# Attention, GLU and SoLU layers on one core: small tiles in a pool of their own, and the next block's q turned earlier from other slots

## The chip, the cores and the metric

The kernel runs on one core of a Trainium2 chip. The metric is the device time of one execution in microseconds (us); before the change the median of three runs is 1464.21 us (1464.13 to 1465.03). A core has TensorE (PE, matrix products; PEld is its loading of the stationary operand), VectorE (DVE), ScalarE (ACT), GpSimd (POOL), and SyncE (SP), whose queue issues nearly all DMA transfers here. A matrix product has a stationary operand ("weights", 128 columns) and a moving operand (up to 512 columns).

## What is computed

Three layers one behind the other, in float32 with float64 weights for the last two:

```python
q_s = exp(q - max(q, axis=-1));  q_s /= sum(q_s, axis=-1) + 1e-9      # q, k, v: 8 x 8 x 576 x 64
k_s = exp(k - max(k, axis=2));   k_s /= sum(k_s, axis=2) + 1e-9
kv  = einsum('bhsd,bhse->bhde', k_s, v)
x   = einsum('bhsd,bhde->bhse', q_s, kv)     # put together as 4608 tokens x 512
g   = x @ w_gate;  y = (g * sigmoid(g) * (x @ w_val)) @ w_out         # 512 -> 1536 -> 512
h   = y @ w_in;    s = h * softmax(h)                                 # 512 -> 1024
out = ((s - mean(s)) / sqrt(var(s) + 1e-6) * g_ln) @ w_out2           # 1024 -> 512
```

Each large product is made of three matrix products: an operand is split into a high and a low part (names ending in h and l), and high·high, high·low and low·high are summed.

## The kernel before

**Stages.** The 4608 tokens are ten blocks (`BLOCKS`): blocks 0 and 1 of 288 tokens run in a start-up stage that a clock of due times orders (until about 190 us), blocks 2 to 8 of 512 tokens and block 9 of 448 run in a hand-written order (`block`, 190 to 1050 us), and the last layer runs over 36 tiles of 128 tokens (`rest`, `emit_h`, `emit_out`, from about 1053 us).

**A block.** It has 36 gaps, three for each of the 12 columns i of w_gate and w_val. In gap 3i stands `emit_g` (12 products `wg`, then Silu on ACT), in gap 3i+1 the output product of the column before (`next_o`, 12 products `y`), in gap 3i+2 `emit_v` (12 products `wv`, then `v_rest`: multiply on DVE, L851; high part on ACT, L855; low part on DVE, L857). The engines work their instructions off in program order. `tasks_of(j)` puts further tasks into the gaps, behind the block's own work of that gap: k and v of the same block j (`kv_load`, `v_load`, `kv_max_rows`, `kv_max_all`, `kv_exp`, `kv_mm`, in two halves of four heads, the second half 12 gaps behind the first), and q of the next block (`q_max` 8, `q_exp` 12, `q_norm` 20, `q_turn` 24, `q_split` 27 to 30, `x_mm` 29 to 32). `x_mm` makes the next block's x in four parts, each of which starts with three or six products `px` (six where the block's tokens lie in two of the eight batches).

**Turning q.** `q_turn` (L647) copies the low and high halves of q's words into the tile `qw` (DVE L652, ACT L653), and a transposing DMA (L655) writes `qwT`, from which `q_split` (L659) puts together z (DVE and ACT, L664) and its parts qh (ACT L669) and ql (DVE L670). `qw` lies in the slot of k (`kt`), `qwT` in that of v (`vt`); both have one buffer, so `q_turn` stands behind the second half's `kv_mm` in gap 23. k, v and q for the next block are loaded together in gap 32 (`load_next`, L765), q by one transfer for each head and batch (16 where a block lies in two batches).

**Weights.** Columns 0 to 4 and 9 to 11 are loaded again for every block by `stream_next` in gap 3f+2, and in gap 25 for column 11 (three slots in turn: a0, a3, a4); each load waits until the products that used its slot are through, and is used nine gaps later. Columns 5 to 8 (`wgv5` to `wgv8`) and all of w_out stay; `wgv4` to `wgv8`, `wo2` and `wo3` were first loaded into tiles b0 to b6 of the pool `wb`, and `wo5` took b0 from `wgv4`. One `wo` tile serves two columns. So of the 432 products of 512 columns in a block, those with weights in `wb` are 4 × 24 for `wgv5` to `wgv8` and 6 × 12 for `wo2`, `wo3` and `wo5`: 168.

**Where the tiles lie.** Pools follow each other in each partition's bytes: const, w, x, a, tmp, att, and behind att first att0, later wb, later late2. Nearly all tiles are multiples of 512 bytes. Behind const's small tiles everything starts at byte 224 modulo 512: all tiles of w, x, a, tmp and those of k, v and q. In att the tiles qm, qs and rs (640 bytes) put qh and ql at 352 modulo 512, and m, r, r2 and r3 (1184 bytes) put z, and all of wb, at 0. In late2 (last layer), nm, se, ss, nmu, sv and rstd put zh and zl at 64. wb starts at byte 170496 of the partition; all tiles at 224 end below 158432.

**y_fix** (L776, blocks 3 to 6) adds two halves of y of the start-up blocks in a tile `fix` in the slot `yt`, which the end of a block's output (`emit_o`, gap 4 of the next block) uses too.

Of the kernel before, what the change touches and what calls it, by code (L numbers as in the profile page):

```python
# [9 lines left out]
F32 = mybir.dt.float32  # L10
# [9 lines left out]
P = 128  # L20
# [97 lines left out]
def attention_glu_solu_kernel(  # L118
# [23 lines left out]
    nc = tc.nc  # L142
# [28 lines left out]

    const = ctx.enter_context(tc.tile_pool(name="const", bufs=1))
    dram = ctx.enter_context(tc.tile_pool(name="dram", bufs=1, space=DRAM))
    wpool = ctx.enter_context(tc.tile_pool(name="w", bufs=1))

    ident = const.tile([P, P], F32, name="ident")
# [246 lines left out]

    def kv_max_rows(pool, b, h0):
        raw = kt_t[b, h0][0]
        km_t[b, h0] = m = pool.tile([SP, HG, D], F32, tag="m", bufs=1, name="m")
        nc.vector.tensor_reduce(
            out=m, in_=raw.rearrange("p c h d -> p h d c"), axis=AX.X, op=ALU.max
        )

    def kv_max_all(pool, b, h0, split=0):

        raw, kt = kt_t[b, h0]
        m = km_t.pop((b, h0))
        kt_sub.add((b, h0))
        N = HG * D
        NQ = SP // 32
        r = pool.tile([SP, N // 32], F32, tag="r", bufs=1, name="r")
        nc.vector.tensor_reduce(
            out=r, in_=m.rearrange("p h (e j) -> p (h e) j", j=32), axis=AX.X, op=ALU.max,  # L440
            apply_transpose=True,
        )
        r2 = pool.tile([32, N // 32, NQ], F32, tag="r2", bufs=1, name="r2")
        for a in range(NQ):
            nc.vector.tensor_copy(out=r2[:, :, a], in_=r[32 * a:32 * (a + 1), :])
        r3 = pool.tile([32, N // 32], F32, tag="r3", bufs=1, name="r3")
        nc.vector.tensor_reduce(out=r3, in_=r2, axis=AX.X, op=ALU.max)
        mb = tmp.tile([SP, N // 32, 32], F32, tag="st", bufs=3, name="mb")
        for a in range(NQ):
            nc.vector.tensor_copy(  # L450
                out=mb[32 * a:32 * (a + 1)],
                in_=r3.rearrange("p (n o) -> p n o", o=1).to_broadcast([32, N // 32, 32]),
            )
        mt = pool.tile([SP, 1, HG, D], F32, tag="m", bufs=1, name="mt")
# [68 lines left out]
    def kv_mm(ps, pool, b, h0, u):  # L523
        kt, vt = kt_t[b, h0][1], vt_t[b, h0]
        pr = h0 // 2 + u
        need(pr in k_done if b == 0 else (b, h0) in kt_exp)
        pk = ps.tile([P, D + 1], F32, tag="gv", name="pk")
        for c in range(KC):
            for a in range(2):
                nc.tensor.matmul(  # L530
                    out=pk[a * D:(a + 1) * D, :],
                    lhsT=kt[:, c, 2 * u + a, :],
                    rhs=vt[:, 2 * u + a, c, 0:D + 1],
                    start=(c == 0),
                    stop=(c == KC - 1),
                )
        yield d["rs"]
        hi, lo = kv_parts[b % 2, pr]
        rs = pool.tile([P, 1], F32, tag="rs", bufs=4, name="rs")
        nc.vector.tensor_scalar_add(out=rs, in0=pk[:, D:D + 1], scalar1=1e-9)  # L540
        nc.vector.reciprocal(out=rs, in_=rs)
        yield d["kvh"]
        diag = [slice(a * D, (a + 1) * D) for a in range(2)]
        for s in diag:
            nc.scalar.activation(out=hi[s, s], in_=pk[s, 0:D], func=AF.Copy, scale=rs[s])
        yield d["kvl"]
        for s in diag:
            nc.vector.scalar_tensor_tensor(
                out=lo[s, s], in0=pk[s, 0:D], scalar=rs[s], in1=f32(hi[s, s]),
                op0=ALU.mult, op1=ALU.subtract,  # L550
            )
        kv_done.add((b, pr))
# [13 lines left out]
    def q_load(pool, j, raw_pool=None, tag="qt"):  # L566
        b, half = divmod(j, 2)
        if j >= 2:
            x = pool.tile([BLOCKS[j][1] // 4, 4, H, D], F32, tag=tag, bufs=1, name=tag)
            for b, s, ps in segments(j):  # L570
                for h in range(H):
                    nc.sync.dma_start(
                        out=x[ps, :, h, :],
                        in_=q[b, h, s:s + 4 * (ps.stop - ps.start), :]
                        .rearrange("(p c) d -> p c d", c=4),
                    )
            qt_t[j] = x, x
            return
        qt_t[j] = heads_load(
# [10 lines left out]
    def q_max(pool, j, hs):  # L590
# [2 lines left out]
        placed(qt_t, j)  # L593
        raw, qt = (t[:, :, hs, :] for t in qt_t[j])
        n, nc_, nh = qt.shape[:3]
        qm = pool.tile([n, nc_, nh, 1], F32, tag="qm", bufs=2, name="qm")
# [10 lines left out]
    def q_norm(pool, j, hs):  # L607
        qt = qt_t[j][1][:, :, hs, :]
        n, nc_, nh = qt.shape[:3]
        qs = pool.tile([n, nc_, nh, 1], F32, tag="qs", bufs=2, name="qs")  # L610
# [36 lines left out]
    def q_turn(pool, j):  # L647

        n = BLOCKS[j][1] // 4
        w = pool.tile([n, 2, 4 * H * D], U16, tag="kt", bufs=1, name="qw")  # L650
        low, high = halves(qt_t[j][1].rearrange("p c h d -> p (c h d)"))
        nc.vector.tensor_copy(out=w[:, 0], in_=low)  # L652
        nc.scalar.copy(out=w[:, 1], in_=high)  # L653
        qw_t[j] = wT = pool.tile([P, 2, 4, NPAIR, n], U16, tag="vt", bufs=1, name="qwT")
        nc.sync.dma_start_transpose(  # L655
            out=wT.rearrange("e w c r p -> e (w c r) p"), in_=w.rearrange("p w n -> p (w n)")
        )
# [65 lines left out]
    def tasks_of(j):  # L723
# [5 lines left out]

        t = {}  # L730
        if j < B:
            for n in range(2):
                g, h0 = 12 * n, n * HG
                if n:
                    at(t, g, kv_load, att, j, h0)
                    at(t, g, v_load, att, j, h0)
                at(t, g + 2, kv_max_rows, att, j, h0)
                at(t, g + 5, kv_max_all, att, j, h0)
                at(t, g + 9, kv_exp, j, h0)
        at(t, 15, conv_w2, j - 2, 3)  # L740
        at(t, 23, conv_w2, j - 2)
        if j < B:
            for n in range(2):
                for u in range(2):
                    at(t, 12 * n + 11, kv_mm, ps_at, att, j, n * HG, u)
        if j + 1 < NB:
            at(t, 8, q_max, att, j + 1, ALLH)
            at(t, 12, q_exp, j + 1, ALLH)
            at(t, 20, q_norm, att, j + 1, ALLH)
            at(t, 24, q_turn, att, j + 1)  # L750
            at(t, 24, x_tiles, ph1x, j + 1)
            for p in range(NPAIR):
                at(t, 27 + p, q_split, att, j + 1, p)
                at(t, 29 + p, x_mm, ps_at, j + 1, p)
            at(t, 32, load_next, j + 1)
        for e, f in enumerate(STREAM):
            if f is not None:
                at(t, 3 * f + 2, stream_next, j, e)
# [3 lines left out]
            y_fix(t, (j - 3) // 2, 2 * ((j - 3) % 2))  # L762
        return t

    def load_next(j):  # L765

        if j + 1 < NB:
            if j < B:
                kv_load(att, j, 0)
                v_load(att, j, 0)  # L770
            q_load(att, j + 1)

    def y_of(j):
# [2 lines left out]
    def y_fix(t, j, d):  # L776
# [12 lines left out]
        def store():  # L789
            nc.sync.dma_start(out=y_of(j)[d:d + 2].rearrange("k p t -> p k t"), in_=tiles[0])  # L790

        at(t, 8, load, 0, y_of(j))
        for c in range(len(FCH) - 1):
            at(t, 8 + 18 * c, load, 1, y_part[j, c])
            at(t, 26 + 18 * c, add)
        at(t, 10 + 18 * (len(FCH) - 1), store)

    acts = {}

# [255 lines left out]
    stream[0] = clock.at(K["go"], products)  # L1055
    with tc.manual_schedule(engines=COMPUTE):
        clock.run()
    load_next(2)
    man = ExitStack()
    man.enter_context(tc.manual_schedule())  # L1060
    for j in range(2, NB - 1):
# [61 lines left out]
        phs[t] = ph  # L1123

    def emit_max(t):
        nm = l2.tile([P, 1], F32, tag="nm", bufs=3, name="nm")
        nc.vector.tensor_reduce(out=nm, in_=phs[t], axis=AX.X, op=ALU.max, negate=True)
        zs[t] = nm

    def emit_e(t):  # L1130
        nm = zs[t]
        e = l2.tile([P, DF2], F32, tag="e", bufs=2, name="e")
        se = l2.tile([P, 1], F32, tag="se", bufs=3, name="se")
        nc.scalar.activation(out=e, in_=phs[t], func=AF.Exp, bias=nm, accum_out=se)
        zs[t] = e, se

    def emit_solu(t):
# [5 lines left out]
        ss = l2.tile([P, 1], F32, tag="ss", bufs=3, name="ss")  # L1143
# [3 lines left out]
        nmu = l2.tile([P, 1], F32, tag="nmu", bufs=3, name="nmu")  # L1147
        nc.vector.tensor_scalar_mul(out=nmu, in0=ss, scalar1=-1.0 / DF2)
        zs[t] = e, nmu

    def emit_square(t):
        e, nmu = zs[t]
        junk = l2.tile([P, DF2], BF16, tag="junk", bufs=1, name="junk")
        sv = l2.tile([P, 1], F32, tag="sv", bufs=3, name="sv")
        nc.scalar.activation(out=junk, in_=e, func=AF.Square, bias=nmu, accum_out=sv)
        zs[t] = e, nmu, sv

    def emit_rstd(t):
# [4 lines left out]
        rstd = l2.tile([P, 1], F32, tag="rstd", bufs=3, name="rstd")  # L1163
        nc.gpsimd.tensor_tensor(out=rstd, in0=sv, in1=neg_half, op=ALU.pow)
        zs[t] = e, nmu, rstd

# [173 lines left out]
```

## Time and profile before

| | us |
|---|---|
| median of three runs | 1464.21 |
| the profiled execution | 1466.67 |
| its span in the trace | 1464.9 |
| start-up stage | 0 to 190 |
| blocks 2 to 9 | 190 to about 1053 |
| last layer | about 1053 to 1464.9 |
| TensorE busy | 1404.7 (96%) |
| VectorE, ScalarE, GpSimd busy | 727.8, 696.1, 143.7 |
| mean granted TensorE clock | 0.984 of full |

The page gives shares over the whole span. What TensorE waited for is read from the view of waits, where in a block it waited from the timeline, and the time from one product's start to the next one's start, which is what a row of products costs, from the timeline too: the ends of products are modelled, the starts are not.

### The profile page before, as it was taken

Reading aid. Unit: us, or ns where it says so; the run is one execution under the profiler, and the core shown is the slowest. Engines: PE = TensorE matmul, PEld = TensorE weight load, DVE = VectorE, ACT = ScalarE, POOL = GpSimd, SP = SyncE. Lnnn points to the kernel's source line nnn. Section 1 sums busy time; section 2 is a strip of 40 time slices with the busy share of each in tenths; the row PEclk is TensorE's granted clock in tenths of the full one; section 3 lists DMA queues with packets and bytes.
Section 4 is the critical chain, followed back from the end, with each engine's and each line's share of the span. In section 5 each row is a group of like instructions: output and inputs, shape, how many; then the busy total and the mean of one; then the engine's idle time right before and its main releaser. Section 6 shows DMA issues by size and latency. Waiting matters only on the chain.

```text
span 1464.9 us, 18454 instructions
## 1 busy us (share of the span) xinstructions
PE 1404.7 (96%) x7263; PEld 1174.2 (80%) x7263; DVE 727.8 (50%) x1220; ACT 696.1 (48%) x927; POOL 143.7 (10%) x112
## 2 busy tenths in 40 slices
PE   7797899999999999999999999999999999999998
PEld 5687888788788788788778788889978888888887
DVE  6767643444444444443444422522257666666663
ACT  6885435425425425425425423422247566566553
POOL 3001202102102102102102100000000000000000
PEclk8899899999999999999999999999999999999999
DMA  9856274374375384385384352464324443444441
GB/s 272 314 164 189 62 204 152 105 209 141 89 227 147 82 241 140 85 243 135 97 231 119 102 179 91 141 232 170 133 66 108 104 98 69 102 103 94 101 79 36
DMA packets 256518, 207.12 MB, mean 141 GB/s; under 512 B 208944, under 2 KB 229424, under 8 KB 244656
## 3 DMA queue, kind: packets, MB, share of 16 engines
q1 hardware_dynamic: 256432, 205.95, 50.3%
q8 instruction: 57, 0.93, 0.3%
q14 instruction: 29, 0.24, 0.0%
HBM read 142.87 MB, written 38.01 MB: 123 GB/s over the span
## 4 chain that ended last, share of the span: by engine, by line
PE 76%; ACT 8%; DVE 6%; DMA 5%; SPq 3%; issue 1%; POOL 0%; ACTq 0%; DVEq 0%; POOLq 0%
PE wg L801 6%; PE wg L802 5%; PE wg L803 5%; PE y L802 5%; PE y L803 5%; PE y L801 5%; PE wv L801 5%; PE wv L802 5%; PE wv L803 5%; PE y L1231 4%; PE y L1230 4%; PE y L1229 4%; PE ph L1119 4%; PE ph L1118 4%; PE ph L1120 4%; DMA qwT<-qw 3%
## 5 line engine op out<-in xcount | busy, mean ns | idle before, releaser
L851 DVE TENSOR_TENSOR st<-st,wv 128x512 f32<-128x512 f32 (+2 forms) x120 | 75.9, 632 | 346.3 <-PE wv L803 318.7
L855 ACT CAST ah<-st 128x512 fp32r<-128x512 f32 (+2 forms) x120 | 70.5, 587 | 353.7 <-DVE st L851 353.7
L801 PE MATMUL y<-ah,wo 128*128 128x512 f32 (+2 forms) x480 | 180.2, 375 | 8.9 <-ACT ah L855 5.7
L802 PE MATMUL y<-al,wo 128*128 128x512 f32 (+2 forms) x480 | 180.3, 376 | 8.5 <-DVE al L857 8.5
L801 PE MATMUL wg<-xh,wgv 128*128 128x512 f32 (+2 forms) x480 | 182.8, 381 | 5.5 <-DVE wgv L256 3.2
L803 PE MATMUL wg<-xh,wgv 128*128 128x512 f32 (+2 forms) x480 | 180.4, 376 | 1.0 <-DVE wgv L258 1.0
L802 PE MATMUL wg<-xl,wgv 128*128 128x512 f32 (+2 forms) x480 | 180.0, 375 | 0.0
L803 PE MATMUL y<-ah,wo 128*128 128x512 f32 (+2 forms) x480 | 179.7, 374 | 0.0
L801 PE MATMUL wv<-xh,wgv 128*128 128x512 f32 (+2 forms) x480 | 179.0, 373 | 0.0
L802 PE MATMUL wv<-xl,wgv 128*128 128x512 f32 (+2 forms) x480 | 178.6, 372 | 0.0
L803 PE MATMUL wv<-xh,wgv 128*128 128x512 f32 (+2 forms) x480 | 178.5, 372 | 0.0
L857 DVE TENSOR_TENSOR al<-st,ah 128x512 fp32r<-128x512 f32 (+2 forms) x120 | 85.6, 714 | 74.6 <-ACT ah L855 74.6
L1231 PE MATMUL y<-w,zl 128*128 128x512 f32 (+1 forms) x296 | 115.6, 390 | 0.4 <-DVE zl L1200 0.3
L1229 PE MATMUL y<-w,zh 128*128 128x512 f32 (+1 forms) x296 | 115.5, 390 | 0.0
L1230 PE MATMUL y<-w,zh 128*128 128x512 f32 (+1 forms) x296 | 115.4, 390 | 0.0
L1118 PE MATMUL ph<-w,yh 128*128 128x512 f32 x288 | 112.8, 392 | 0.0
L1119 PE MATMUL ph<-w,yh 128*128 128x512 f32 x288 | 112.7, 391 | 0.0
L1120 PE MATMUL ph<-w,yl 128*128 128x512 f32 x288 | 112.4, 390 | 0.0
L802 PEld LDWEIGHTS y<-al,wo 128*128 128x128 f32 x480 | 92.0, 192 | 24.9 <-DVE al L857 9.9
L801 PEld LDWEIGHTS y<-ah,wo 128*128 128x128 f32 x480 | 91.8, 191 | 25.2 <-ACT ah L855 6.2
L846 ACT ACTIVATE st<-wg 128x512 f32<-128x512 f32 (+2 forms) x120 | 67.1, 559 | 92.2 <-PE wg L803 91.4
L801 PEld LDWEIGHTS wg<-xh,wgv 128*128 128x128 f32 x480 | 91.8, 191 | 21.9 <-issue 3.5
(239 smaller groups left out, 2423.5 us busy)
## 6 DMA issues: line engine op xcount, KB each, us to landing
wgv<-w_dram SPq DMA_DIRECT2D x64, 1024.0 KB, 5.5
vt<-in_v_dram SPq DMA_DIRECT2D x64, 144.0 KB, 4.7
yr<-y_dram SPq DMA_DIRECT2D x9, 1024.0 KB, 6.4
w_dram<-wgv SPq DMA_DIRECT2D x8, 1024.0 KB, 8.3
w_dram<-w2r SPq DMA_DIRECT2D x8, 1024.0 KB, 4.3
w<-w_dram SPq DMA_DIRECT2D x8, 1024.0 KB, 4.9
kt<-in_k_dram SPq DMA_DIRECT2D x56, 144.0 KB, 5.7
out_dram<-ot SPq DMA_DIRECT2D x58, 128.0 KB, 2.4
```

The source lines that it names most:

```text
L801: nc.tensor.matmul(out=po, lhsT=wh, rhs=rh, start=start, stop=False)
L802: nc.tensor.matmul(out=po, lhsT=wh, rhs=rl, start=False, stop=False)
L803: nc.tensor.matmul(out=po, lhsT=wl, rhs=rh, start=False, stop=stop)
L851: nc.vector.tensor_tensor(out=st, in0=st, in1=pv, op=ALU.mult)
L855: nc.scalar.copy(out=ah, in_=st)
L857: nc.vector.tensor_tensor(out=al, in0=st, in1=f32(ah), op=ALU.subtract)
L1118: nc.tensor.matmul(out=po, lhsT=yh[:, kk, s], rhs=wh, start=(kk == 0), stop=False)
L1119: nc.tensor.matmul(out=po, lhsT=yh[:, kk, s], rhs=wl, start=False, stop=False)
L1120: nc.tensor.matmul(out=po, lhsT=yl[:, kk, s], rhs=wh, start=False, stop=(kk == KD - 1))
L1229: nc.tensor.matmul(out=po[:, s], lhsT=zh[:, c, :], rhs=wh[:, s], start=first, stop=False)
L1230: nc.tensor.matmul(out=po[:, s], lhsT=zh[:, c, :], rhs=wl[:, s], start=False, stop=False)
L1231: nc.tensor.matmul(out=po[:, s], lhsT=zl[:, c, :], rhs=wh[:, s], start=False, stop=last)
```

## The change

A pool `stat` at the other end of the partition's bytes (`side="right"`) takes the small tiles m, r, r2, r3, rs, qm, qs and, in the last layer, nm, se, ss, nmu, sv, rstd. With these gone every tile left in att, att0, wb and late2 in front of which they stood moves to byte 224 modulo 512 (wb now starts at 168672).

From block 3 on, `qw` takes the slot `yt` and `qwT` the slot of q itself. `q_norm` goes from gap 20 to 14 and `q_turn` from 24 to 18. The second half of k and v goes from gaps 14, 17, 21, 23 to 17, 20, 24, 26 (its loads stay in 12). `load_next` is cut in two: k and v are loaded in gap 27, q in gap 33 (behind the weights of gap 32, ahead of those of 35), by four transfers a batch, one for each quarter c of the tokens. `y_fix` loads in gap 6, adds in 11 and stores in 12 (before: 8, 26, 28).

```diff
+    stat = ctx.enter_context(tc.tile_pool(name="stat", bufs=1, side="right", reuse_waits="tile"))
...
-        rs = pool.tile([P, 1], F32, tag="rs", bufs=4, name="rs")
+        rs = stat.tile([P, 1], F32, tag="rs", bufs=4, name="rs")
...
             for b, s, ps in segments(j):
-                for h in range(H):
-                    nc.sync.dma_start(
-                        out=x[ps, :, h, :],
-                        in_=q[b, h, s:s + 4 * (ps.stop - ps.start), :]
-                        .rearrange("(p c) d -> p c d", c=4),
-                    )
+                rows = q[b, :, s:s + 4 * (ps.stop - ps.start), :].rearrange(
+                    "h (p c) d -> p c h d", c=4
+                )
+                for c in range(4):
+                    nc.sync.dma_start(out=x[ps, c], in_=rows[:, c])
...
-        w = pool.tile([n, 2, 4 * H * D], U16, tag="kt", bufs=1, name="qw")
+        (wp, wt), tt = ((pool, "kt"), "vt") if j == 2 else ((tmp, "yt"), "qt")
+        w = wp.tile([n, 2, 4 * H * D], U16, tag=wt, bufs=1, name="qw")
...
-        qw_t[j] = wT = pool.tile([P, 2, 4, NPAIR, n], U16, tag="vt", bufs=1, name="qwT")
+        qw_t[j] = wT = pool.tile([P, 2, 4, NPAIR, n], U16, tag=tt, bufs=1, name="qwT")
...
-            for n in range(2):
-                g, h0 = 12 * n, n * HG
+            for n, (load, rows, sub, exp, mm) in enumerate(((0, 2, 5, 9, 11), (12, 17, 20, 24, 26))):
+                h0 = n * HG
...
-            at(t, 20, q_norm, att, j + 1, ALLH)
-            at(t, 24, q_turn, att, j + 1)
+            at(t, 14, q_norm, att, j + 1, ALLH)
+            at(t, 18, q_turn, att, j + 1)
...
-            at(t, 32, load_next, j + 1)
+            at(t, 27, kv_next, j + 1)
+            at(t, 33, q_next, j + 1)
...
-        at(t, 8, load, 0, y_of(j))
-        for c in range(len(FCH) - 1):
-            at(t, 8 + 18 * c, load, 1, y_part[j, c])
-            at(t, 26 + 18 * c, add)
-        at(t, 10 + 18 * (len(FCH) - 1), store)
+        need(len(FCH) == 2)
+        at(t, 6, load, 0, y_of(j))
+        at(t, 6, load, 1, y_part[j, 0])
+        at(t, 11, add)
+        at(t, 12, store)
```

## Rows read from the trace of the kernel before

**Rows 1.** Page, part 1 (busy us) and part 2 (granted clock in 40 slices).

```profile
PE 1404.7 (96%) x7263; PEld 1174.2 (80%) x7263; DVE 727.8 (50%) x1220; ACT 696.1 (48%) x927; POOL 143.7 (10%) x112
...
PEclk8899899999999999999999999999999999999999
```

**Rows 2.** Waits of TensorE: total us, times, longest us.

```profile
PE px L693 <- ACT qh L669: 12.1, 7, 2.0
...
PE wg L801 <- DMA wgv<-w_dram: 2.4, 3, 1.1
```

**Rows 3.** Timeline of TensorE, block 2 (start us, us, engine, line, operation, out<-in).

```profile
284.16 0.39 PE L803 MATMUL wv<-xh,wgv 128*128 128x512 f32 x1
...
287.91 0.40 PE L801 MATMUL wg<-xh,wgv 128*128 128x512 f32 x1
...
295.69 0.39 PE L803 MATMUL y<-ah,wo 128*128 128x512 f32 x1
...
296.87 0.39 PE L801 MATMUL wv<-xh,wgv 128*128 128x512 f32 x1
```

**Rows 4.** Timeline of TensorE, the first of these places in block 7.

```profile
833.54 0.39 PE L803 MATMUL wv<-xh,wgv 128*128 128x512 f32 x1
...
837.31 0.45 PE L801 MATMUL wg<-xh,wgv 128*128 128x512 f32 x1
```

**Rows 5.** Timeline of VectorE, block 3, gaps 23 to 28.

```profile
378.22 0.69 DVE L857 TENSOR_TENSOR al<-st,ah 128x512 fp32r<-128x512 f32 x1 [0.68 <-ACT ah L855]
...
381.95 0.15 DVE L540 TENSOR_SCALAR rs<-pk 128x1 f32<-128x1 f32 x1
...
384.79 0.58 DVE L548 SCALAR_TENSOR_TENSOR kvl<-pk,rs,kvh 64x64 fp32r<-64x64 f32 x2 [0.76 <-ACT kvh L545]
...
395.37 0.45 DVE L664 COPY z<-qwT 128x512 uint16<-128x512 uint16 x1 [4.87 <-DMA qwT<-qw]
396.81 0.69 DVE L670 TENSOR_TENSOR ql<-z,qh 128x512 fp32r<-128x512 f32 x1 [0.99 <-ACT qh L669]
```

**Rows 6.** Timeline of ScalarE, the same stretch.

```profile
384.77 1.28 ACT L846 ACT_TABLE_LOAD   x1
386.06 0.60 ACT L846 ACTIVATE st<-wg 128x512 f32<-128x512 f32 x1
```

**Rows 7.** Timeline of SP's queue, block 3, the transposing DMA.

```profile
388.61 4.79 SPq L655 DMA_TRANSPOSE qwT<-qw  x1
```

**Rows 8.** A window with a low granted clock: length, busy us (x instructions) of each engine, PEclk.

```profile
288.50:291.90 3.40, 3.40 (x10) 2.62 (x9) 2.72 (x5) 1.77 (x3) 0.00 (x0) 0.50 0.86 342
```

**Rows 9.** Timeline of SP's queue, end of block 4 and start of block 5.

```profile
519.75 11.54 SPq L572 DMA_DIRECT2D qt<-in_q_dram x16
531.39 4.68 SPq L280 DMA_DIRECT2D wgv<-w_dram x3
```

**Rows 10.** Timeline of TensorE, block 3: 48 products (columns 2, 3), 36 (column 7), kv_mm.

```profile
330.62 0.39 PE L801 MATMUL wv<-xh,wgv 128*128 128x512 f32 x1
...
341.28 0.39 PE L803 MATMUL wv<-xh,wgv 128*128 128x512 f32 x1
...
368.17 0.40 PE L801 MATMUL wg<-xh,wgv 128*128 128x512 f32 x1
...
376.34 0.40 PE L803 MATMUL wv<-xh,wgv 128*128 128x512 f32 x1
376.67 1.62 PE L530 MATMUL pk<-vt,kt 96*64 96x65 f32 x48
```

**Rows 11.** Timeline of TensorE, last layer: 18 of the products ph, 24 products y.

```profile
1254.96 0.39 PE L1118 MATMUL ph<-w,yh 128*128 128x512 f32 x1
...
1258.81 0.39 PE L1120 MATMUL ph<-w,yl 128*128 128x512 f32 x1
1259.04 0.39 PE L1229 MATMUL y<-w,zh 128*128 128x512 f32 x1
...
1264.65 0.39 PE L1118 MATMUL ph<-w,yh 128*128 128x512 f32 x1
```

More of the change, by code (lines that the diff above doesn't have):

```diff
@@ L425, in kv_max_rows @@
         raw = kt_t[b, h0][0]
-        km_t[b, h0] = m = pool.tile([SP, HG, D], F32, tag="m", bufs=1, name="m")
+        km_t[b, h0] = m = stat.tile([SP, HG, D], F32, tag="m", bufs=1, name="m")
         nc.vector.tensor_reduce(
@@ L437, in kv_max_all @@
         NQ = SP // 32
-        r = pool.tile([SP, N // 32], F32, tag="r", bufs=1, name="r")
+        r = stat.tile([SP, N // 32], F32, tag="r", bufs=1, name="r")
         nc.vector.tensor_reduce(
@@ L442, in kv_max_all @@
         )
-        r2 = pool.tile([32, N // 32, NQ], F32, tag="r2", bufs=1, name="r2")
+        r2 = stat.tile([32, N // 32, NQ], F32, tag="r2", bufs=1, name="r2")
         for a in range(NQ):
             nc.vector.tensor_copy(out=r2[:, :, a], in_=r[32 * a:32 * (a + 1), :])
-        r3 = pool.tile([32, N // 32], F32, tag="r3", bufs=1, name="r3")
+        r3 = stat.tile([32, N // 32], F32, tag="r3", bufs=1, name="r3")
         nc.vector.tensor_reduce(out=r3, in_=r2, axis=AX.X, op=ALU.max)
@@ L453, in kv_max_all @@
             )
-        mt = pool.tile([SP, 1, HG, D], F32, tag="m", bufs=1, name="mt")
+        mt = stat.tile([SP, 1, HG, D], F32, tag="m", bufs=1, name="mt")
         nc.vector.transpose(
@@ L595, in q_max @@
         n, nc_, nh = qt.shape[:3]
-        qm = pool.tile([n, nc_, nh, 1], F32, tag="qm", bufs=2, name="qm")
+        qm = stat.tile([n, nc_, nh, 1], F32, tag="qm", bufs=2, name="qm")
         nc.vector.tensor_reduce(out=qm[:, :, :, 0], in_=raw, axis=AX.X, op=ALU.max)
@@ L609, in q_norm @@
         n, nc_, nh = qt.shape[:3]
-        qs = pool.tile([n, nc_, nh, 1], F32, tag="qs", bufs=2, name="qs")
+        qs = stat.tile([n, nc_, nh, 1], F32, tag="qs", bufs=2, name="qs")
         nc.vector.tensor_reduce(out=qs[:, :, :, 0], in_=qt, axis=AX.X, op=ALU.add)
@@ L731, in tasks_of @@
         if j < B:
-            for n in range(2):
-                g, h0 = 12 * n, n * HG
+            for n, (load, rows, sub, exp, mm) in enumerate(((0, 2, 5, 9, 11), (12, 17, 20, 24, 26))):
+                h0 = n * HG
                 if n:
[L735 to L739, printed above, removed]
+                    at(t, load, kv_load, att, j, h0)
+                    at(t, load, v_load, att, j, h0)
+                at(t, rows, kv_max_rows, att, j, h0)
+                at(t, sub, kv_max_all, att, j, h0)
+                at(t, exp, kv_exp, j, h0)
+                for u in range(2):
+                    at(t, mm, kv_mm, ps_at, att, j, h0, u)
         at(t, 15, conv_w2, j - 2, 3)
         at(t, 23, conv_w2, j - 2)
[L742 to L745, printed above, removed]
         if j + 1 < NB:
@@ L763, in tasks_of, with kv_next, q_next @@
         return t
-    def load_next(j):
+    def kv_next(j):
+        if j < B:
+            kv_load(att, j, 0)
+            v_load(att, j, 0)
+    def q_next(j):
         if j + 1 < NB:
-            if j < B:
-                kv_load(att, j, 0)
-                v_load(att, j, 0)
             q_load(att, j + 1)
@@ L1057, in attention_glu_solu_kernel @@
         clock.run()
-    load_next(2)
+    kv_next(2)
+    q_next(2)
     man = ExitStack()
@@ L1125, in emit_max @@
     def emit_max(t):
-        nm = l2.tile([P, 1], F32, tag="nm", bufs=3, name="nm")
+        nm = stat.tile([P, 1], F32, tag="nm", bufs=3, name="nm")
         nc.vector.tensor_reduce(out=nm, in_=phs[t], axis=AX.X, op=ALU.max, negate=True)
@@ L1132, in emit_e @@
         e = l2.tile([P, DF2], F32, tag="e", bufs=2, name="e")
-        se = l2.tile([P, 1], F32, tag="se", bufs=3, name="se")
+        se = stat.tile([P, 1], F32, tag="se", bufs=3, name="se")
         nc.scalar.activation(out=e, in_=phs[t], func=AF.Exp, bias=nm, accum_out=se)
@@ L1142, in emit_solu @@
         nc.vector.reciprocal(out=se, in_=se)
-        ss = l2.tile([P, 1], F32, tag="ss", bufs=3, name="ss")
+        ss = stat.tile([P, 1], F32, tag="ss", bufs=3, name="ss")
         nc.vector.scalar_tensor_tensor(
@@ L1146, in emit_solu @@
         )
-        nmu = l2.tile([P, 1], F32, tag="nmu", bufs=3, name="nmu")
+        nmu = stat.tile([P, 1], F32, tag="nmu", bufs=3, name="nmu")
         nc.vector.tensor_scalar_mul(out=nmu, in0=ss, scalar1=-1.0 / DF2)
@@ L1153, in emit_square @@
         junk = l2.tile([P, DF2], BF16, tag="junk", bufs=1, name="junk")
-        sv = l2.tile([P, 1], F32, tag="sv", bufs=3, name="sv")
+        sv = stat.tile([P, 1], F32, tag="sv", bufs=3, name="sv")
         nc.scalar.activation(out=junk, in_=e, func=AF.Square, bias=nmu, accum_out=sv)
@@ L1162, in emit_rstd @@
         )
-        rstd = l2.tile([P, 1], F32, tag="rstd", bufs=3, name="rstd")
+        rstd = stat.tile([P, 1], F32, tag="rstd", bufs=3, name="rstd")
         nc.gpsimd.tensor_tensor(out=rstd, in0=sv, in1=neg_half, op=ALU.pow)
```

## The prediction

> **What bounds the kernel now.** I read the page first: TensorE is busy for 96% of the span, the next engine for half of it, and the clock is full in nearly all slices past the first five [rows 1]. So a gain must come from one of three places: TensorE's idle time, low clock, or the time from one product to the next. The waits name two idle causes that this change touches: px waits for qh, 12.1 us in seven waits, and wg waits for a load of weights, 2.4 us in three [rows 2]. Then I went to the timeline for the rate. In block 3 the 48 products from 330.62 to 341.28 start 47 intervals apart, 10.66 / 47 = 226.8 ns each; the 36 products of column 7, from 368.17 to 376.34, are 8.17 / 35 = 233.4 ns apart [rows 10]. Both are the same three lines over the same x; what differs is the tile that holds the weights: a-tiles at byte 224 modulo 512, as x is, in the first stretch, b-tiles at byte 0 in the second. The last layer shows the same pair: 17 intervals of the products ph (both operands at 224) take 3.85 us, 226.5 ns each, and the 24 products y, whose stationary zh and zl lie at 64 and whose moving weights at 224, take 1264.65 - 1259.04 = 5.61 us, 233.8 ns each [rows 11]. That VectorE and ScalarE are half idle and that the rate holds over whole runs of products without a wait says that the 6.6 ns lie in TensorE's own reading.
>
> **The change part by part.** All sums are made against the profiled execution: 1466.67 us, its span 1464.9 with 1.8 around it. The median of the runs, 1464.21, is 2.46 below that execution; I take the same gain off the median.
>
> *One byte modulo 512.* The diff takes 640, 1184 and (last layer) 576 bytes of small tiles out of the row, and all that is left are multiples of 512. So weights and moving operand lie at 224 in every 512-column product. In a block 168 of 432 products have weights in wb, 7 blocks of 512 columns: 1176 products, each 233.4 - 226.8 = 6.6 ns: 7.8 us. In the last layer 35 of the 36 tiles have 24 such products y (the last one is cut in halves): 840, each 233.8 - 226.8 = 7.0 ns: 5.9 us. Together 13.7 us. The blocks of 288 and 448 columns I leave at nothing: a part k of their x starts at k × 1152 or k × 1792 bytes, so it is not at one byte with the weights before or after. DVE and ACT instructions on the moved tiles I also leave at nothing: these engines stand idle half of the time. The bounds are nothing (the byte is not the cause, see the rivals) and these 13.7 us; a loss is excluded, since the first stretch of rows 10 is the state that all products get.
>
> *q turned at gap 18.* Now the two halves are copied behind the second kv_mm; the transposing DMA is issued at 388.61 and q_split's first copy can start at 395.37, after 4.87 us in which DVE idles: the DMA takes 395.37 - 388.61 = 6.8 us [rows 5, 7]. TensorE pays in the first of the four px: in block 2 it is 287.91 - 284.16 = 3.75 us from the product before px to the one behind it, at the third px, which waits for nothing, 296.87 - 295.69 = 1.18 us [rows 3], so 2.57 us; in block 7 837.31 - 833.54 = 3.77 us [rows 4], 2.59 us by the same measure. There are six such blocks, 2 to 7: 6 × 2.6 = 15.6 us. With the turn six gaps earlier (72 products, 72 × 0.227 = 16.3 us) the data is there 16.3 - 4.9 = 11 us ahead of the first copy's place. What is late next: q_split now stands behind the second kv_mm of gap 26. Counted from the end of gap 26's wv (376.67 in the row of kv_mm, where it stood in gap 23), v_rest ends 378.22 + 0.69 - 376.67 = 2.2 us later; the tail of kv_mm on DVE, from rs to the last kvl, takes 384.79 + 0.58 - 381.95 = 3.4 us [rows 5, 10]; ScalarE has its table load and Silu behind its last part of that, 1.28 + 0.60 = 1.9 us [rows 6], and z, qh and ql take 396.81 + 0.69 - 395.37 = 2.1 us [rows 5]. Laid end to end, with ScalarE free for Silu 0.6 us ahead of DVE's last kvl: 2.2 + 3.4 - 0.6 + 1.9 + 2.1 = 9.0 us. Meanwhile TensorE has kv_mm, 1.6 us [rows 10], and the products of gaps 27 to 29, 36 × 0.227 = 8.2 us, before it comes to px: 9.8 us. It fits by 0.8 us, and I count the whole 15.6 us; the other bound is 1.5 us left over in each of six blocks, 9 us. What moves to gaps 14 to 20 (q_norm, the copies, the transposing DMA with 4.79 us of SP's queue [rows 7]) has v_rest and Silu queued behind it on DVE and ACT, which idle for half of a block, and on SP the load of gap 25; the load of gap 14, ahead of it, is needed in gap 30.
>
> *The low clock.* Behind three of these six stalls the clock is granted at half (1.2 instead of 2.4 GHz) for 3.4 us: at 288.5, 397.7 and 838.0; in such a stretch 10 products run, the first and last in part, instead of 15 [rows 8]. Each costs at most half of 3.4 us, 1.7; part of one is in the px above; I take 1.4 us each, 4.2 us, gone when the stall in front of it is gone. Bounds: 0 and 5.1.
>
> *Loads.* Now 16 transfers of q hold SP's queue for 11.54 us, and three loads of weights are issued only at 531.39 [rows 9]; column 1 of the next block waits for the first of them. Behind the change column 1's load (gap 32) goes ahead of q. The three waits, 2.4 us [rows 2], go. k and v are issued five gaps earlier, ahead of column 0's load, whose slot is free only at the end of gap 29; it has six gaps, 16 us. Column 2's load (gap 35) stands behind q's four to eight transfers: if these hold SP as long as the 16 do now, it is issued near gap 37 and must be there by gap 42: 13 us. Cost 0; the slower rival has the other bound.
>
> *Nothing:* y_fix earlier (one add on DVE in gap 11 instead of 26; its loads wait on SP for the store of yt, with only a load due at gap 8 behind them), x_tiles, the start-up stage (the same tasks).
>
> Sum: 13.7 + 15.6 + 4.2 + 2.4 = 35.9 us; span 1464.9 - 35.9 = 1429.0, profiled execution 1430.8, median 1464.2 - 35.9 = **1428.3 us**.
>
> **The page that speaks against it.** Rows 10 and 11 show two rates that go with the byte of the weights' tile. The Trainium skill, SBUF — State Buffer, section "SBUF: two separate sides", says that TensorE never waits for another engine's accesses, and TensorE: Matmul & The Clock Gate, Part 2, that loading the next weights takes no read bandwidth from the running product. By these the place of a tile should not matter and the 13.7 us would not come: 1442.0. The trace doesn't agree with a single rate, but it does not prove the byte either; that is the first rival.
>
> **The rivals.** *The byte is not the cause (0.13).* Every slow tile lies above byte 170496, every fast one below 158432; place and byte can't be told apart in this trace. If it is the place in the memory, or something else that goes with wb and late2, the tiles stay there and nothing is gained: 1428.3 + 13.7 = 1442.0. For the byte speaks that slow rates come with two different bytes (0 and 64) and in both roles of the operands.
>
> *A new wait takes the place of the DMA (0.15).* The chain behind gap 26 fits by 0.8 us only. If it takes 1.5 us longer, px waits 0.7 us in six blocks: 1432.5; with half of the stalls and the low clocks left, 1428.3 + 7.8 + 4.2 = 1440.3.
>
> *The turn doesn't come earlier (0.03).* qw waits in slot yt for y_fix's store or for that of the last block; then stalls and low clock stay: 1428.3 + 15.6 + 4.2 = 1448. Against it: between those stores (gaps 12 and 4) and the copies lie 6 and 14 gaps, 16 and 38 us.
>
> *Slower (0.03).* q's transfers have four times the rows of before. If each held SP four times as long as one does now (4 × 11.54 / 16 = 2.9 us [rows 9]) and a block in two batches has eight, q takes 23 us from the start of gap 33; column 2's load, with 6.8 us to land as the longer bound [rows 5, 7], then comes 29.8 us behind that point, and is needed after nine gaps, 24.5 us: 5.3 us late. The point from which it loses anything is 17.7 us of q; to lose the 35.9 us it takes 6 us in each of six blocks, so q over 24 us; at 30 us it is 1428.3 + 6 × 12.3 = 1502. Against it: the bytes are the same, and 16 issues in 11.54 us show that no transfer is awaited before the next.
>
> **How the numbers follow.** Forecast 0.66, its own range 1422 to 1434: above it 4.2 us of low clock or part of the px term may stay. With the first two rivals it reaches 1442. Below, 6 us are kept for what a smoother block gives beyond the sum. Range 1422 to 1442. What a measurement can tell from no change is about 0.2%, 3 us. Faster 0.95 (all but the last rival and a mixture of misses), same 0.02, slower 0.03.
>
> **What would show it.** In the profile after: products in column 7 and in y of the last layer 226.8 ns apart as in the others; no wait of px for qh above 0.5 us and no idle of DVE for qwT in blocks 2 to 7; no window at half clock between 200 and 1060 us; no wait of wg for a load. Wrong would make it: 233 ns still in wb's products; px waiting for kvl or ql in place of the DMA; SP's q transfers lasting over 18 us; wg of column 2 waiting at the start of a block.

## The result and the profile after

| | before | after |
|---|---|---|
| median, us | 1464.17 (1462.98 to 1465.03, 4 runs) | 1428.59 (1426.38 to 1428.78, 4 runs) |
| the profiled execution, us | 1466.67 | 1428.78 |
| its span, us | 1464.9 | 1426.9 |
| first 512-column product to first product ph, us | 188.39 to 1050.70: 862.3 | 188.78 to 1018.79: 830.0 |
| first turning product to last product of the last layer, us | 1067.02 to 1460.76: 393.7 | 1035.19 to 1422.72: 387.5 |

After stands to before as 0.9754 (95% interval 0.9737 to 0.9771). The medians are 35.6 us apart, the spans 38.0; the forecast was 35.9 us and 1428.3 us. The blocks gave 32.3 us, the last layer 6.2 us. The rest of the span took half a microsecond more.

From the page of after: part 1, the row of the granted clock in part 2, and the shares of the chain that ended last in part 4.

```profile
PE 1384.3 (97%) x7263; PEld 1174.8 (82%) x7263; DVE 728.1 (51%) x1220; ACT 695.2 (49%) x927; POOL 143.8 (10%) x112
...
PEclk9899899999999999999999999999999999999999
...
PE 85%; ACT 7%; DVE 5%; DMA 1%; issue 1%; POOL 0%; SPq 0%; ACTq 0%; DVEq 0%; POOLq 0%
```

Against [rows 1], the other engines do the same work in the same time (VectorE 728.1 against 727.8 us), and TensorE does the same 7263 products in 20.4 us less busy time. So 20.4 of the 38.0 us are not idle time that was removed but products that take less time, by their rate or by the clock. The waits of after, TensorE's for qh and VectorE's for the transposing DMA (total us, times, longest):

```profile
PE px L695 <- ACT qh L671: 1.3, 1, 1.3
...
DVE z L666 <- DMA qwT<-qw: 4.8, 1, 4.8
```

Before it was seven waits and 12.1 us for qh [rows 2]. The one that is left lies at the end of the start-up stage, where q is still turned as before. No wait of wg for a load is left.

**The rate.** TensorE's timeline of after: in block 3, first and last of 24 products in a row, 12 with weights in `wo3` and 12 in `wgv8` (both in the pool wb); then in the last layer the first of 24 products y and the product behind the last of them.

```profile
373.74 0.39 PE L805 MATMUL y<-ah,wo 128*128 128x512 f32 x1
...
378.95 0.39 PE L807 MATMUL wv<-xh,wgv 128*128 128x512 f32 x1
...
1224.35 0.39 PE L1234 MATMUL y<-w,zh 128*128 128x512 f32 x1
...
1229.79 0.39 PE L1123 MATMUL ph<-w,yh 128*128 128x512 f32 x1
```

23 intervals take 5.21 us, 226.5 ns each, where column 7's products were 233.4 ns apart [rows 10]; 24 intervals take 5.44 us, 226.7 ns, where y had 233.8 [rows 11]. Over all such products of the trace, weights in wb went from 233.2 ns to 226.7, y of the last layer from 233.9 to 226.8, and the products that were fast before gained some tenths of a nanosecond each (0.4 in the blocks, 0.9 among the products ph).

**The chain ahead of px.** Block 4 of after, around its first px: TensorE; then VectorE and ScalarE's last steps of the chain; then SP's queue.

```profile
493.84 0.39 PE L807 MATMUL wv<-xh,wgv 128*128 128x512 f32 x1
494.07 0.25 PE L695 MATMUL px<-qh,kvh 128*128 128x192 f32 x1
...
494.84 0.40 PE L805 MATMUL wg<-xh,wgv 128*128 128x512 f32 x1
```

```profile
485.77 0.69 DVE L861 TENSOR_TENSOR al<-st,ah 128x512 fp32r<-128x512 f32 x1 [0.69 <-ACT ah L859]
...
489.21 0.58 DVE L550 SCALAR_TENSOR_TENSOR kvl<-pk,rs,kvh 64x64 fp32r<-64x64 f32 x2 [0.76 <-ACT kvh L547]
489.82 0.47 DVE L666 COPY z<-qwT 128x512 uint16<-128x512 uint16 x1
492.57 0.69 DVE L672 TENSOR_TENSOR ql<-z,qh 128x512 fp32r<-128x512 f32 x1 [2.28 <-ACT qh L671]
```

```profile
490.49 0.60 ACT L850 ACTIVATE st<-wg 128x512 f32<-128x512 f32 x1
491.11 0.78 ACT L666 COPY z<-qwT 128x512 uint16<-128x512 uint16 x1
```

```profile
466.06 4.88 SPq L657 DMA_TRANSPOSE qwT<-qw  x1
...
494.26 10.85 SPq L282 DMA_DIRECT2D wgv<-w_dram  x2
505.21 6.71 SPq L577 DMA_DIRECT2D qt<-in_q_dram  x8
```

The transposing DMA is issued at 466.06, 23.8 us ahead of the first copy of z at 489.82, which waits for nothing now. The six gaps were to bring the data 11 us ahead of that place; it is there about 17 us ahead (23.8 less the 6.8 that the DMA took before). From the last kvl the chain goes through Silu and the copy on ScalarE to ql, which ends at 492.57 + 0.69 = 493.26; TensorE reaches px at 494.07. The slack is 0.8 us. The six px take 494.84 - 494.07 = 0.77 us without a hole, and in all six blocks the first px takes what the third takes. Before, the first px took 2.58, 3.19, 2.55, 2.68, 2.83 and 2.72 us longer than the third, 16.5 us together. The eight transfers of q hold SP for 6.71 us, where sixteen held it for 11.54 [rows 9].

### The profile page after: what moved, and what is told of

Read it like the earlier page. It is cut to its first block, busy times and chain, and to the rows that moved or that the text cites. A ratio compares the mean times of both kernels' runs of the same rounds, so it can differ in the third digit from the quotient of the medians.

```text
span 1426.9 us, 18380 instructions
## 1 busy us (share of the span) xinstructions
PE 1384.3 (97%) x7263; PEld 1174.8 (82%) x7263; DVE 728.1 (51%) x1220; ACT 695.2 (49%) x927; POOL 143.8 (10%) x112
## 4 chain that ended last, share of the span: by engine, by line
PE 85%; ACT 7%; DVE 5%; DMA 1%; issue 1%; POOL 0%; SPq 0%; ACTq 0%; DVEq 0%; POOLq 0%
PE wg L805 6%; PE y L806 6%; PE y L807 6%; PE y L805 6%; PE wv L805 6%; PE wv L807 6%; PE wv L806 6%; PE wg L807 6%; PE wg L806 6%; PE y L1236 4%; PE y L1235 4%; PE y L1234 4%; PE ph L1123 4%; PE ph L1125 4%; PE ph L1124 4%; PE pk L532 1%
## 5 line engine op out<-in xcount | busy, mean ns | idle before, releaser
L805 PE MATMUL wg<-xh,wgv 128*128 128x512 f32 (+2 forms) x480 | 180.2, 375 | 3.2 <-DVE wgv L258 3.2
L807 PE MATMUL wg<-xh,wgv 128*128 128x512 f32 (+2 forms) x480 | 178.2, 371 | 0.7 <-DVE wgv L260 0.7
L1234 PE MATMUL y<-w,zh 128*128 128x512 f32 (+1 forms) x296 | 113.6, 384 | 0.0
L1235 PE MATMUL y<-w,zh 128*128 128x512 f32 (+1 forms) x296 | 113.5, 383 | 0.0
```

The source lines that it names most:

```text
L805: nc.tensor.matmul(out=po, lhsT=wh, rhs=rh, start=start, stop=False)
L807: nc.tensor.matmul(out=po, lhsT=wl, rhs=rh, start=False, stop=stop)
L1234: nc.tensor.matmul(out=po[:, s], lhsT=zh[:, c, :], rhs=wh[:, s], start=first, stop=False)
L1235: nc.tensor.matmul(out=po[:, s], lhsT=zh[:, c, :], rhs=wl[:, s], start=False, stop=False)
```

## The experiments

**Bytes alone.** Before, with the pool `stat` and nothing else of the change:

```diff
+    stat = ctx.enter_context(tc.tile_pool(name="stat", bufs=1, side="right", reuse_waits="tile"))
...
-        rs = pool.tile([P, 1], F32, tag="rs", bufs=4, name="rs")
+        rs = stat.tile([P, 1], F32, tag="rs", bufs=4, name="rs")
...
```

> The kernel before with the pool stat alone: all tiles at byte 224 modulo 512, the order of before. By the sum of the prediction it saves 13.7 us: 1450.5 us, with products of column 7 and of the last layer's y 226.8 ns apart and the six stalls ahead of px, the low clocks and the waits for loads still there. If the rate came with the new order and not with the byte, it stays at 1464.

Median 1455.89 us (1453.53 to 1457.99) against 1465.15 (1458.96 to 1471.12) for the kernel before beside it, ratio 0.9942 (0.9917 to 0.9967): 9.3 us, not 13.7. The rate did what was expected: all products in the blocks and y of the last layer start 226.8 ns apart, and the last layer is 6.1 us shorter (5.9 expected). The blocks are only 4.5 us shorter (186.78 to 1044.56, 857.8 us). TensorE's wait for qh shows where the rest went, and so do two stretches of the clock (length, busy us and instructions of PE, PEld, DVE, ACT and POOL, granted clock, DMA share, GB/s):

```profile
PE px L694 <- ACT qh L670: 13.7, 7, 2.3
```

```profile
283.80:287.20 3.40, 3.40 (x10) 2.88 (x11) 1.72 (x4) 2.01 (x4) 0.00 (x0) 0.50 0.66 190
393.00:399.80 6.80, 6.40 (x18) 5.21 (x18) 4.35 (x8) 3.78 (x6) 0.00 (x0) 0.50 0.76 236
```

The DMA lasts as long as before (issued at 274.78, z copied from 281.52: 6.7 us). But between gap 23, where the chain to the DMA starts, and px lie 48 products with weights in wb, 0.3 us shorter now: TensorE comes to px earlier and waits longer, 19.1 us over the six blocks by the measure above, against 16.5 (some of that is half clock already; idle alone is 14.6 against 12.9). And half clock now stands behind all six stalls, where it stood behind three, one stretch of double length. Stall and half clock together are read from the product ahead of the first px to the product ahead of the second px, less the same stretch at the third: 20.7 us before, 28.6 here.

One more difference lies at the very start. The count of the blocks begins at a px at the end of the start-up stage, and before has a stretch at half clock just behind it that this run has not; first before, then this run:

```profile
189.50:192.90 3.40, 3.40 (x15) 3.31 (x14) 2.32 (x5) 3.00 (x7) 0.00 (x0) 0.50 0.81 160
```

```profile
189.50:192.90 3.40, 3.24 (x21) 2.76 (x20) 2.66 (x6) 2.77 (x6) 0.00 (x0) 1.00 0.54 86
```

From block 2's first wg, which lies behind it, to the first ph it is 850.2 us before, 846.7 here and 817.9 in after. As a sum for these 3.5 us: 1176 products by 6.5 ns and 0.9 us for the other products, 8.5 us off; the rows that waited for loads, 2.9 off (2.4 of it idle [rows 2]); stalls and half clock, 28.6 - 20.7 = 7.9 on: 3.5 us. The part is worth its full price only where nothing in the block is bound by another engine. No wait of wg for a load was left here either, though sixteen transfers of q still went ahead of the weights.

**Order alone.** After, with the small tiles back in their old pools (the same lines, undone):

```diff
-        rs = stat.tile([P, 1], F32, tag="rs", bufs=4, name="rs")
+        rs = pool.tile([P, 1], F32, tag="rs", bufs=4, name="rs")
...
```

> The changed kernel without the pool stat: the tiles lie as before, the new order stays. By the sum of the prediction it gives back 13.7 us of the gain: 1428.6 + 13.7 = 1442.3 us, products with weights in wb 233.4 ns apart, no stall ahead of px. If the two parts shared a gain, the two savings of this run and of e1_bytes would not add up to 35.6 us.

Median 1442.51 us (1440.56 to 1443.04), ratio 0.9853 (0.9823 to 0.9883): 22.6 us against the kernel before beside it, 22.2 forecast. No wait ahead of px and no low clock in the blocks, but the slow rate is back; block 3, column 8:

```profile
377.24 0.40 PE L804 MATMUL wv<-xh,wgv 128*128 128x512 f32 x1
...
379.81 0.40 PE L806 MATMUL wv<-xh,wgv 128*128 128x512 f32 x1
```

11 intervals, 2.57 us, 233.6 ns each. So the bytes, laid on the new order, are worth 1442.51 - 1428.59 = 13.9 us; on the old order 9.3. The two parts are not additive: 22.6 + 9.3 = 31.9, together 35.6. The runs of the kernel before beside these two spread over 12 us, so that the medians alone would not show this. The traces do: from block 2's first wg to the first ph the order alone saves 23.7 us (826.5) and the bytes alone 3.5, both 32.3. The stall and the low clock couple them.

**The modulus.** After, with pads that shift the tiles of wb, and zh and zl, by different amounts against x and the w tiles:

```diff
         for n, x in enumerate(mid):
+            pad = (0, 32, 32, 32, 32, 64, 64)[n]
+            if pad:
+                z = w_b.tile([P, pad // 4], F32, tag=f"pad{n}", name="pad")
+                nc.gpsimd.memset(z, 0.0)
             load_w1(w_b, f"b{n}", *x)
...
+        if t == 0:
+            z1 = l2.tile([P, 64], F32, tag="pad1", bufs=1, name="pad")
...
+        if t == 0:
+            z2 = l2.tile([P, 16], F32, tag="pad2", bufs=1, name="pad")
```

> The changed kernel with empty tiles of 32 and 64 bytes between the weights of wb, so that they lie 0 (wo5), 32 (wgv5), 64 (wo2), 96 (wgv6), 128 (wgv7), 192 (wo3) and 256 bytes (wgv8) off the moving operand's byte modulo 512, and with zh 256 and zl 320 bytes off the moving weights in the last layer. All lie where the fast ones of the changed kernel lie, so place alone makes all 226.7 ns. If one byte modulo 512 is needed, all but wo5 go to about 233. If a smaller step is enough (before, 288 and 352 bytes off were slow, and in the block of 448 columns 256 off was as fast as 0), 32 and 96 are slow and the rest keep 226.7 with a step of 64; with a step of 128, 64, 192 and 320 are slow too.

One run, 1435.32 us (span 1433.4). TensorE's timeline in block 3: column 7's wv at 128 bytes from the moving operand, wg of column 8 at 256, an output with `wo3` at 192, wv of column 8 at 256. (The output in gap 3i+1 is that of column i-2, not of the column before.)

```profile
367.79 0.39 PE L805 MATMUL wv<-xh,wgv 128*128 128x512 f32 x1
...
370.58 0.39 PE L805 MATMUL wg<-xh,wgv 128*128 128x512 f32 x1
...
373.31 0.39 PE L805 MATMUL y<-ah,wo 128*128 128x512 f32 x1
...
376.06 0.39 PE L805 MATMUL wv<-xh,wgv 128*128 128x512 f32 x1
...
378.56 0.39 PE L807 MATMUL wv<-xh,wgv 128*128 128x512 f32 x1
```

12 intervals at 128 take 2.79 us (232.5 ns), 12 at 192 take 2.75 (229.2), 11 at 256 take 2.50 (227.3). Over all seven blocks:

| weights less moving operand, bytes modulo 512 | from one product to the next, ns | seen in |
|---|---|---|
| 0 | 226.8 to 227.3 | a-tiles, and `wo5` above byte 168672 |
| 32 | 232.9 | `wgv5` |
| 64 | 233.6 | `wo2` |
| 96 | 233.9 | `wgv6` |
| 128 | 232.3 | `wgv7` |
| 192 | 229.2 | `wo3` |
| 256 | 227.2 (last layer 228.2) | `wgv8`, zh |
| 288 | 233.2 | wb of the kernel before |
| 320 | 235.6 | zl |
| 352 | 233.8 | zh and zl of the kernel before |

The rate goes with the byte at which the weights lie, and it repeats after 256: 256 is as good as 0, and 288, 320 and 352 are as bad as 32, 64 and 96. It isn't a step at one size; 192 lies a third of the way. In all these products the moving operand lies at 224 modulo 512, so no run tells whether the distance between the two counts or the weights' own byte. As a sum: a block's 24 products at each of 32, 64, 96, 128 and 192, by their excess over 226.8, are 0.67 us, 4.7 in seven blocks; in the last layer 16 products at 228.2 and 8 at 235.6 are 0.09 us, 3.2 over 35 tiles. 7.9 us were to be lost. The run lies 6.7 us above the median of after (1435.32 - 1428.59), and 8.3 to 8.6 us above the two runs beside it in which px hardly waits either, 1426.73 and 1427.02 (below).

The table holds for 512 columns alone. In the block of 448 columns the same tiles stand in another order: wg of column 8 (256 bytes off), an output with `wo3` (192 off), then wv of column 8:

```profile
990.30 0.36 PE L805 MATMUL wg<-xh,wgv 128*128 128x448 f32 x1
...
992.73 0.36 PE L805 MATMUL y<-ah,wo 128*128 128x448 f32 x1
...
995.13 0.37 PE L805 MATMUL wv<-xh,wgv 128*128 128x448 f32 x1
```

12 intervals take 2.43 us at 256 off, but 2.40 at 192. By the starts within a row of 12, products lie 202.4 to 203.1 ns apart at 0 and 256, 204.5 to 204.8 at 32, but 201.1 to 201.5 at 96 and 199.8 to 200.3 at 192: the bytes that are slow with 512 columns are the fastest here. Products of 288 columns are 132.6 ns apart in before and after alike.

**The turn back at gap 24, the new slots kept.**

```diff
-            at(t, 18, q_turn, att, j + 1)
+            at(t, 24, q_turn, att, j + 1)
```

> The changed kernel with q_turn in gap 24 again, in its new slots. If the gap is what removed the stall, px waits again in six blocks: about 1428.6 + 15.6 = 1444 us or more. If the slots are (qw no longer waits for kv_mm to free k's slot), the transposing DMA can start about gap 25.5 and be there at gap 28, behind which q_split's chain of 2 to 3 us ends about when TensorE comes to px: within 2 us of 1428.6.

Median 1429.16 us (1427.59 to 1429.43), ratio 0.9764: the same as after. VectorE still waits for the DMA in every block, though 19.1 us in all where before had 38.5; TensorE hardly does. VectorE's wait, and TensorE in block 6, the first px and the second:

```profile
DVE z L666 <- DMA qwT<-qw: 19.1, 8, 4.8
```

```profile
703.68 0.39 PE L807 MATMUL wv<-xh,wgv 128*128 128x512 f32 x1
703.98 0.41 PE L695 MATMUL px<-qh,kvh 128*128 128x320 f32 x1
704.71 0.42 PE L696 MATMUL px<-ql,kvh 128*128 128x320 f32 x1 [0.31 <-DVE ql L672]
...
705.42 0.41 PE L805 MATMUL wg<-xh,wgv 128*128 128x512 f32 x1
```

In blocks 2 to 5 the first px is as short as the third; in blocks 6 and 7 it is 0.8 us longer (here 705.42 - 703.68 = 1.74 against 0.98). The six gaps themselves are worth 2 × 0.8 us in the trace and 0.6 in the medians, less than the times can tell.

What the copies stand behind shows why. VectorE in block 3, in the kernel before (the copy that rows 5 leave out, behind the last kvl, which ends at 385.37), then in this run, and this run's SP queue:

```profile
385.40 1.23 DVE L652 COPY qw<-qt 128x2048 uint16<-128x2048 uint16 x1
```

```profile
377.17 1.22 DVE L654 COPY qw<-qt 128x2048 uint16<-128x2048 uint16 x1
...
382.20 0.15 DVE L542 TENSOR_SCALAR rs<-pk 128x1 f32<-128x1 f32 x1
```

```profile
379.99 5.57 SPq L657 DMA_TRANSPOSE qwT<-qw  x1
```

Before, the copy follows the tail of kv_mm (rs to kvl) at once; VectorE was busy, and no wait for the slot shows. Here it stands ahead of that tail, which went with kv_mm from gap 23 to 26, and the DMA is issued 9.7 us ahead of the product in front of px (389.67), where before had 6.1 (388.61 to 394.74). The new slots are what lets the copies go first: in the slot of k they could not be written before kv_mm had read k. But with kv_mm left in gap 23 they would still stand behind its tail in program order, whatever their slot. No run has the one without the other, so that both are needed is argued, not shown.

**How much slack the chain has.** ScalarE's first copy of z done once more, and four times more; the additional copies write what is there already:

```diff
+        if j > 2 and pr == 0:
+            for _ in range(1):      # range(4) in the second kernel
+                nc.scalar.copy(
+                    out=halves(z)[1].rearrange("e (c p) -> e c p", c=4), in_=wT[:, 1, :, pr, :]
+                )
```

> The changed kernel in which ScalarE makes its copy of the first z of a block once more (0.78 us): the chain from kv_mm to ql grows from 9.0 to 9.8 us, as long as TensorE's work ahead of px. px waits at most 0.1 us in a block, within 1 us of 1428.6. If the chain had no slack, it would cost 0.8 us in each of six blocks.

> The same copy four times more, 3.1 us: less the slack of 0.8 us px waits 2.3 us in each of six blocks, 14 us in all: 1442 us. If a stall of this length is what lowers the clock, windows at half clock come back behind some of the six (three did behind stalls of 2.6 us), up to 1.5 us each; if not, the clock stays full in the blocks.

One more copy, 0.78 us: one run, 1427.02 us; the first px takes 0.00 to 0.05 us longer than the third. The slack that the prediction worked out, 0.8 us, is there and it is just used up. Four more, 3.1 us: one run, 1448.4 us, where 1442 was expected. TensorE's wait, and the granted clock behind the last of the six stalls:

```profile
PE px L700 <- ACT qh L676: 10.5, 7, 1.6
```

```profile
826.70:830.10 3.40, 3.40 (x10) 2.64 (x9) 2.05 (x4) 1.92 (x4) 0.00 (x0) 0.50 0.35 140
```

The first px is 2.37 to 2.67 us longer than the third in each of six blocks, 15.0 us (14 expected). The rest is the clock: half clock behind five of the six (all but block 6). From block 2's first wg to the first ph it is 840.6 us, 22.7 more than after; 22.7 - 15.0 = 7.7 us for five stretches, some 1.5 us each. The prediction took 1.4 us, and this is where the 6 us above the expectation come from.

**The place of the loads.** After, with k, v and q all loaded in gap 32 ahead of the weights, as before, but q still by four transfers a batch:

```diff
-            at(t, 27, kv_next, j + 1)
-            at(t, 33, q_next, j + 1)
+            at(t, 32, kv_next, j + 1)
+            at(t, 32, q_next, j + 1)
```

> The changed kernel with k, v and q loaded in gap 32 ahead of column 1's weights, as before, but q in its four transfers a batch. If the place in the queue removed the waits of wg for loads, column 1 of the next block waits again, about 1 us in some of the blocks, 2.4 us in all. If the fewer transfers did (6.7 instead of 11.5 us of SP for q), wg waits for no load.

One run, 1426.73 us, within the runs of after. SP's queue at the end of block 4:

```profile
492.62 2.96 SPq L389 DMA_DIRECT2D kt<-in_k_dram  x4
495.63 3.89 SPq L415 DMA_DIRECT2D vt<-in_v_dram  x4
499.63 7.70 SPq L577 DMA_DIRECT2D qt<-in_q_dram  x8
507.43 12.73 SPq L282 DMA_DIRECT2D wgv<-w_dram  x3
```

Column 1's weights are issued behind q, at 507.43 at the earliest, where after has them issued by 494.26 + 10.85 = 505.11, ahead of q; still wg waits for no load. The place in the queue was not what the change needed.

**The low clock at the start of the last layer.** Behind the start of block 2, after has one stretch at half clock left before its last product, at 1036.6, behind a wait of TensorE for e (before has the same at 1066.7). A kernel that has the next tile's products ph ahead of it:

```diff
     emit_h(1)
-    rest(1, turn=0)
     emit_h(2)
+    rest(1, turn=0)
     emit_out(0)
```

> The changed kernel with the 24 products ph of tile 2 put ahead of the turning of tile 0 at the start of the last layer. There TensorE waits 2.9 us for VectorE's scaled e, and the clock falls to half behind it for 3.4 us. The third tile's products fill that wait: about 3 us off the wait and 1 to 2 us off the low clock, 1424 us. If the turning is late anyway (the copies of zh and zl queued behind tile 1's work), it stays within 1 us of 1428.6.

Median 1428.37 us (1427.62 to 1429.09), ratio 0.9761: no gain. The wait of after, and then what stands at this place in the new kernel:

```profile
1035.19 1.09 PE L1215 MATMUL y<-ident,e 128*128 128x128 f32 x8 [2.89 <-DVE e L1174]
```

```profile
1032.98 0.50 PE L1123 MATMUL ph<-w,yh 128*128 128x512 f32 x1 [1.45 <-ACT yh L1092]
...
1040.12 0.50 PE L1234 MATMUL y<-w,zh 128*128 128x512 f32 x1 [0.24 <-ACT zh L1219]
...
1070.51 0.50 PE L1234 MATMUL y<-w,zh 128*128 128x512 f32 x1 [0.90 <-ACT zh L1203]
```

The 2.89 us and the low clock are gone, but from the first ph to the last product it is 404.1 us, in after 403.9. The new kernel waits 1.45 us for yh and 0.24 for zh, and at the hundredth product of 512 columns it is 1.2 us ahead of after; it has given this back behind 1070.51, where it waits 0.90 us for zh and 0.53 for zl in place of 0.43 for zl. That the other engines' softmax steps set the time here, whichever product stands where, fits this, but no run made them shorter. The half clock is not bound to the wait: the run with the turn at gap 24 has the same wait of 2.89 us for e and full clock behind it, and takes 402.4 us from the first ph, 1.5 less than after.

## Why the forecast came out right, and where its reasons did not

**The bytes: the size and the cause right, the modulus too strict.** 13.7 us were forecast, 13.9 measured on the new order. The first rival, that the place above byte 170496 is to blame, falls: wb still lies above 168672 and runs at 226.7 ns, and the padded kernel has fast and slow tiles next to each other there. But "one byte modulo 512" asks for more than the rows of the runs do: 256 bytes between the operands cost nothing in the blocks, and with 448 columns other bytes than the same one are the fastest. The 448-column block was left at nothing on the ground that its parts lie at many bytes; its products with weights in wb went from 204.4 to 202.7 ns, some 0.3 us in all, and the other products of the blocks gained 0.6 us. The 288-column blocks, left at nothing too, show no change. The prediction set a page against this term. The Trainium skill, SBUF — State Buffer, section "SBUF: two separate sides", keeps TensorE clear of other engines' accesses; nothing here speaks against that. The Trainium skill, TensorE: Matmul & The Clock Gate, Part 2, has the loading of the next weights take no read bandwidth from the running product; this leaves no room for a rate that goes with the weights' byte, and for these float32 products the traces have one, 226.8 ns at a distance of 0 and 233.9 at 96: the measurement decides. Whether it is the loading that slows the product no run showed.

**The px term: size right, reason half wrong.** 15.6 us were forecast, 16.5 by the same measure over all six blocks (it held two against one third px, 2.57 and 2.59; each against its own, they run from 2.55 to 3.19, and the 3.19 has some of a stretch at half clock in it). The step "with the turn six gaps earlier" named the wrong part: the turn from gap 24 lost 0.6 us in the medians. What the run at gap 24 shares with after is that the copies of q no longer stand behind the tail of kv_mm, by the new slots together with kv_mm's move to gap 26. What was late next was named rightly, and its slack was right to 0.1 us: one more copy uses it up. Four make the chain 3.1 - 0.8 = 2.3 us late and px 2.4 to 2.7 us late: that is the second rival, which would have come true with a chain that much longer.

**The low clock: size right, the coupling missed.** 4.2 us were forecast. Of the 20.7 us that stall and half clock cost together before, 16.5 are px: 4.2 for three stretches. After has none behind px in blocks 2 to 7; its stretch at 1036.6 belongs to the last layer. The 32.3 us of the blocks come out as 20.7, 7.6 for the bytes (1176 × 6.5 ns), 0.9 for the other products and 2.9 for the rows that waited for loads: 32.1. But the sum treated the parts as independent. With the bytes alone the stall grew and half clock came behind three more stalls, and from block 2's first wg on the blocks gained 3.5 us instead of 7.8.

**The loads: 2.4 us gone, the reason not shown.** The prediction laid it to the weights going ahead of q. Four transfers a batch do as well from the old place. That the kernel with bytes alone had no such wait with sixteen says little: before, the three waits stand at column 1 behind just those three px stalls that no half clock followed (blocks 4 to 6), and with the bytes alone half clock followed all six; it brings TensorE to column 1 later by 1.6 us, more than the longest wait, 1.1 us. With the loads in gap 32 column 1's weights are issued 15.6 us behind the product ahead of px (491.79), where before it was 26.3 (505.10 to 531.39). Which of the fewer transfers, the earlier transposing DMA and the shorter stall gave this, no run separates.

**The last rivals.** The turn did come earlier, and q's eight transfers hold SP for 6.71 us, far below the 17.7 from which it would have cost anything: 0.84 us for each, where one of a quarter of the rows took 0.72.

**What stays open:** what decides whether half clock follows a stall. TensorE's idle time ahead of px was 2.03 to 2.30 us before, and half clock followed 2.13, 2.11 and 2.20 but not 2.03, 2.16 and 2.30; it followed all six of 2.36 to 2.59 with the bytes alone, and five of six of 1.84 to 1.99 with four copies. The 2.89 us for e were followed by it in after and not in the run with the turn at gap 24. Length alone doesn't order these.

## What to carry to other kernels

Where a row of equal products has two rates without a wait, compare the bytes at which weights and moving operand lie in the partition before looking elsewhere, and measure each width of product by itself; small tiles in a pool of their own keep the large ones in step. Where a transfer stands late, ask first what the copies that feed it stand behind, and which buffer holds them there; six gaps of order alone gave next to nothing here. And don't add up a faster rate and a removed stall as if each stood alone: on a stage that waits for another engine, a faster product first makes the wait longer.

## What the runs showed of the hardware that was not expected

A 512-column product with float32 weights took 226.8 ns from start to start with weights and moving operand at the same byte modulo 256, 232.3 to 233.9 ns 32 to 128 bytes off (235.6 for zl at 320), and 229.2 ns 192 bytes off; the moving operand lay at 224 modulo 512 throughout. With 448 columns the order was another: 202.7 ns at 0, 204.5 to 204.8 at 32, 199.8 to 200.3 at 192. A stall of TensorE of about 2 us between dense rows of products was enough for a stretch of 3.4 us at half clock behind it, in some blocks and not in others, and each such stretch cost 1.4 to 1.6 us. Eight transfers of q held SP's queue for 6.7 us and sixteen with the same bytes for 11.5.
